# ScalarE takes the last low words and all high-part casts, early softmax sums go two units at a time, and one FFN stage changes its rank

## The chip, the core and the metric

The kernel runs on one core of a Trainium2 chip. Its time is the device time of one execution, in microseconds; a kernel is told by the median of several. Engines: PE (TensorE) multiplies, DVE (VectorE), ACT (ScalarE) and POOL (GpSimd) work on elements, SP (SyncE) issues nearly all DMAs. Each engine takes its instructions strictly in the order of its own queue, so an instruction that waits holds up everything behind it.

## The reference

Windowed attention, then a feed-forward net (FFN) with a rational activation:

```
scores = q @ k.T / 8 + bias        # batch 4, heads 8, 768 positions, head_dim 64; bias falls with distance
keep   = first 8 keys, or the 96 last positions before the query
a      = softmax(where(keep, scores, -1e9))
x      = (a @ v) as (3072 tokens, 512)
h      = x @ w_in                  # 512 x 2048
g      = (a0 + a1 h + a2 h^2 + a3 h^3) / (1 + |b0||h| + |b1|h^2 + 1e-6)
out    = g @ w_out                 # 2048 x 512
```

The weights lie in memory as 64-bit numbers.

## The kernel before

**Tiling.** The 3072 tokens are 12 chunks of 256. A chunk has 8 attention units (two heads of 128 tokens; u = 0 to 95) and 8 FFN steps (256 of the 2048 hidden columns; f = 0 to 95). Attention runs ahead of the FFN: step f of the FFN stands some 10 to 13 units behind.

**An attention unit.** Transposes of q and k (L385), copies out of PSUM (L396), scores (L428), mask and row maximum on DVE (L461), the exponential with its row sums on ACT (L471), then `st_sums`: two tiny DVE instructions, a sum of the two partial sums of each head (L476) and a reciprocal (L478). POOL divides the row by it (`st_norm`, L487; units 0 to 7 don't, their factor is multiplied in at L551). PE transposes the result (`tp`, L503), ACT copies it out (L506), PE multiplies with v (L529), and ACT and DVE make x (L550 and L551 for chunk 0, L558 and L559 after). Units 0 to 23 (`PLAIN = 24`) go in pairs and in plain fp32; the units behind them go one by one. The sums of four units lie side by side in the tile `stats`.

**An FFN step.** PE makes `h` (L263 in fp32 for chunk 0, L271 with high and low parts for the others) in one of two PSUM banks. ACT reads `h` three times (`ew1`, L295 to L297: tiles fu, fa, fs), DVE twice (`ew2`, L302 and L303, into fu), and POOL adds fa and fs (L304). ACT makes a reciprocal q by logarithm and exponential (`ew3`, L311, L312), DVE finishes fu (`ew4`, L316 to L318), and PE multiplies it with w_out (`ffn2`, L342 for chunk 0, L347 after). The two PSUM banks tie the steps: `h` of step f+2 can only start when L297 and L303 of step f have read theirs.

**Weights.** They come in 32 pieces of 128x512 numbers, 16 of w_in (w1_...) and 16 of w_out (w0_...). A DMA (L183) brings a piece's two 32-bit words into a raw buffer `r...`; there are six such buffers, so the piece six later is fetched when the last reader, L209, is done. `decode` makes fp32 of it: ACT takes the magnitude of the top word (L202), POOL the bits that the low word adds (L206; on ACT, L204, where the piece's number is in `LOW_A`, which is piece 0 alone), and DVE puts them together (L207) and sets the sign (L209). The first 20 pieces keep the magnitude in a PSUM bank (`m0` to `m19`), the last 12 in SBUF. Chunk 0 uses the fp32 pieces. For the other chunks `split_w` makes a rounded high part (L222: on DVE for the 16 even numbers in `HI_V`, on ACT for the 16 odd ones) and a low part by subtraction (L223, on POOL or DVE).

**What sets the order.** A scheduler places the instructions when the program is built: `on` and `ffn` give every stage a place 1000 t + PRI_A[stage] (PRI from chunk 1 of the FFN on), smaller first, and a model of the engines' times decides among what is ready. Within a turn t, decoding has 1850 and `ew2` has 2400.

Of the kernel before, what the change touches and what calls it, by code (L numbers as in the profile page):

```python
# [15 lines left out]
ALU = mybir.AluOpType  # L16
# [18 lines left out]
PLAIN = 24  # L35
# [4 lines left out]

SPLITS = {4: 0, 5: 2, 6: 4, 7: 8, 8: 12, 9: 16, 10: 19, 11: 22, 12: 25, 13: 28, 14: 32}

LOW_A = (0,)
BANKS = "hrhaa" * 2 + "raa" * 3 + "r" + " " * 12
HI_V = (0, 2, 4, 6, 8, 10, 12, 14, 16, 18, 20, 22, 24, 26, 28, 30)
LO_V = (13, 15, 17, 19, 21, 23, 25, 27, 29, 31)


PRI = dict(load=0, score=50, soft=100, sums=120, ffn1a=150, qkT=200, pv=250, qkE=300, x=350, split=400, ew3=450, norm=500,
           ffn1b=550, ew1=600, ew4=650, ew2=700, ffn2a=750, pT=800, ffn2b=850, dec=900, wsplit=990)  # L50
PRI_A = dict(PRI, ffn1a=800, pv=1250, qkT=-150, qkE=-100, sums=950, x=1300, split=-700, ew3=2400, norm=1800, ffn1b=900, ew1=1050,
             ew4=850, ew2=2400, ffn2a=-400, pT=850, ffn2b=2050, dec=1850, wsplit=1090)


def positions(nc, rel, key, q0, k0):
# [51 lines left out]
def tile_kernel(ctx: ExitStack, tc: tile.TileContext, q, k, v, n_global, n_local,  # L107
                w_in, w_out, ca, cb, out):
    nc = tc.nc
# [49 lines left out]
    full = {}  # L159
    hi = {}  # L160

    def piece(dt, key):
        return wide.tile([P, 2 * TOK], dt, tag="w", name=f"w{'_'.join(map(str, key))}{'f' if dt is F32 else 'h'}",
                         bufs=NCT * DF // (2 * TOK) + NFT + 1)

    def w_lo(key):
        if key[0]:
            return win_l[:, key[1], key[2] * 2 * TOK:(key[2] + 1) * 2 * TOK]
        return wout_l[:, key[1], :]
# [15 lines left out]
    def decode(key):  # L185
# [16 lines left out]
        nc.scalar.activation(out=mag, in_=raw[:, :, 1], func=AF.Abs, scale=2.0 ** -112)  # L202
        if n in LOW_A:
            nc.scalar.activation(out=low, in_=half, func=AF.Copy, scale=2.0 ** -13, bias=FLOOR)  # L204
# [14 lines left out]

    def split_w(key):  # L220
        hi[key] = piece(FR, key)
        (nc.vector.tensor_copy if len(hi) - 1 in HI_V else nc.scalar.copy)(out=hi[key], in_=full[key])  # L222
        (nc.vector if len(hi) - 1 in LO_V else nc.gpsimd).tensor_tensor(  # L223
            out=w_lo(key), in0=full[key], in1=hi[key], op=ALU.subtract)

# [10 lines left out]
    stats = const.tile([P, 4, 8], F32, name="stats")  # L236
# [135 lines left out]
    prob = {}  # L372
# [99 lines left out]
                                 accum_out=st[:, 2 + 2 * x:3 + 2 * x])  # L472

    def st_sums(u):
        st = prob[u][1]
        nc.vector.tensor_reduce(out=st[:, 6:8], in_=st[:, 2:6].rearrange("p (x w) -> p x w", w=2), op=ALU.add,  # L476
                                axis=mybir.AxisListType.X)
        nc.vector.reciprocal(out=st[:, 6:8], in_=st[:, 6:8])  # L478

    def st_norm(u):  # L480
        if u < DIVIDED:
# [83 lines left out]
    def windowed(lates):  # L565
# [37 lines left out]
        for t in range(NU + LAG + F2 + 1):  # L603
# [5 lines left out]
            def on(name, fn, u, *args, ffn=False, more=0):  # L609
                if 0 <= u < NU:  # L610
                    tc.cur_priority = int(base + when[ffn] + pri[ffn][name] + more)
                    fn(u, *args)
# [9 lines left out]
            def behind(n):  # L622
                past = t - n - 1
                return [past] if past >= PLAIN else [t - 1, t] if t % 2 and t < PLAIN else []
# [9 lines left out]
            for u in behind(1):  # L634
                on("score", st_score, u)
                on("soft", st_soft, u)
                on("sums", st_sums, u)
            if t == PLAIN:
                scope.close()
                pl.late = lates.enter_context(tc.tile_pool(name="late", bufs=1))  # L640
# [41 lines left out]
            if step:  # L682
                for n, key in enumerate(list(full)[SPLITS.get(f - 1, 0):SPLITS.get(f, 0)]):
                    tc.cur_priority = int(base + when[True] + pri[True]["wsplit"] + 4 * n)
                    split_w(key)
# [95 lines left out]
    with ExitStack() as es:  # L781
        pl.ldp = es.enter_context(tc.tile_pool(name="ldp", bufs=2))
        pl.att = es.enter_context(tc.tile_pool(name="att", bufs=2))
        pl.ffn = es.enter_context(tc.tile_pool(name="ffn", bufs=2))
        pl.ps_h = es.enter_context(tc.tile_pool(name="ps_h", bufs=2, space=PSUM))
        pl.ps_o = es.enter_context(tc.tile_pool(name="ps_o", bufs=2, space=PSUM))
        pl.ps_r = es.enter_context(tc.tile_pool(name="ps_r", bufs=1, space=PSUM))
        pl.ps_t = es.enter_context(tc.tile_pool(name="ps_t", bufs=3, space=PSUM))
        with ExitStack() as lates:
            windowed(lates)  # L790
# [53 lines left out]
```

## Time and profile before

| | |
|---|---|
| median of 3 runs | 755.57 us (755.1 to 756.39) |
| the profiled execution | 755.76 us, its span 754.0 us (1.76 us lie around it) |
| busy: PE, DVE, ACT, POOL | 723.2, 600.8, 570.2, 452.6 us |
| granted TensorE clock, mean | 0.986 |

The profiled execution lies 0.19 us above the median. A busy PE is not PE at its peak, and idle time of an engine that is not the bottleneck costs nothing. In the trace the numbers of tiles are left out: `w_2f` of an L263 is w1_0_2f to w1_3_2f, `fu` any of fu0 to fu95.

### The profile page before, as it was taken

What the parts mean: (1) busy time and instruction counts of PE and PEld (TensorE: products, weight loads), DVE (VectorE), ACT (ScalarE), POOL (GpSimd) and SP (SyncE); (2) the same over time, 40 slices, a digit from 0 to 9 for tenths busy, and PEclk for the clock granted to TensorE, in tenths of its full rate; (3) what the DMA queues carried; (4) which work ended last, traced back from release to release, by engine and by line L of the source; (5) the groups of instructions that cost most, each with busy time, mean ns of one, the idle gap of its engine ahead of it and who ended that gap; (6) DMA issues with size and microseconds to landing.
All of it is one profiled execution on the core that took longest, in us unless ns stands there. A gap on an engine that the chain in (4) does not pass through costs nothing.

```text
span 754.0 us, 15278 instructions
## 1 busy us (share of the span) xinstructions
PE 723.2 (96%) x5026; PEld 626.1 (83%) x5026; DVE 600.8 (80%) x1435; ACT 570.2 (76%) x1253; POOL 452.6 (60%) x498
## 2 busy tenths in 40 slices
PE   5898799999999999999999999999999999999996
PEld 3574466888888988998998998998988989998995
DVE  6889955779788798878788888888888888876665
ACT  5888466787887878878877878877878877875764
POOL 3377676776577566656557666665666575664441
PEclk9998899999999999999999999999999999999998
DMA  9986100114433534434434333433434433210000
GB/s 266 341 266 196 35 23 21 50 44 111 135 99 103 144 101 119 124 102 103 120 98 129 101 100 113 121 106 91 127 92 122 117 99 98 81 50 1 29 2 33
DMA packets 123581, 79.49 MB, mean 105 GB/s; under 512 B 82532, under 2 KB 104036, under 8 KB 123492
## 3 DMA queue, kind: packets, MB, share of 16 engines
q1 hardware_dynamic: 122288, 77.89, 36.1%
q8 instruction: 42, 0.69, 0.4%
q10 hardware_dynamic: 1204, 0.52, 0.3%
q14 instruction: 47, 0.39, 0.2%
HBM read 35.92 MB, written 6.29 MB: 56 GB/s over the span
## 4 chain that ended last, share of the span: by engine, by line
PE 85%; DVE 6%; ACT 3%; DMA 2%; issue 2%; POOL 1%; SPq 1%; POOLq 0%; ACTq 0%; DVEq 0%
PE h L271 32%; PE acc L347 31%; PE o L529 5%; PE s L448 4%; PE h L263 3%; PE tp L503 3%; PE acc L342 3%; PE tk L385 2%; PE s L428 2%; DMA r<-in_moe_w_in_dram 1%; ACT pr L471 1%; DVE pr L461 1%; ACT m L202 1%; DVE m L207 1%; DVE fu L316 0%
## 5 line engine op out<-in xcount | busy, mean ns | idle before, releaser
L487 POOL TENSOR_SCALAR pr<-pr,stats 128x256 f32<-128x256 f32 (+1 forms) x176 | 155.3, 895 | 93.1 <-DVE stats L478 47.8
L271 PE MATMUL h<-xh,win_l 128*128 128x256 f32 x704 | 198.2, 281 | 0.0
L304 POOL TENSOR_TENSOR fa<-fa,fs 128x512 f32<-128x512 f32 x95 | 123.8, 1303 | 82.1 <-ACT fs L297 75.0
L347 PE MATMUL acc<-wout_l,g 128*128 128x512 f32 x352 | 139.5, 396 | 0.0
L327 POOL TENSOR_TENSOR g<-fu,g 128x512 fp32r<-128x512 f32 x87 | 112.8, 1297 | 43.8 <-ACT g L326 29.1
L271 PEld LDWEIGHTS h<-xh,win_l 128*128 128x128 f32 x704 | 133.1, 189 | 2.0 <-issue 1.0
L295 ACT ACTIVATE fu<-h,coef 128x512 f32<-128x512 f32 (+1 forms) x97 | 75.1, 774 | 46.5 <-PE h L271 37.4
L471 ACT ACTIVATE pr<-pr,stats 128x256 f32<-128x256 f32 (+1 forms) x192 | 92.7, 485 | 22.6 <-DVE stats L461 21.8
L302 DVE TENSOR_TENSOR fu<-fu,h 128x512 f32<-128x512 f32 (+1 forms) x97 | 65.7, 677 | 40.5 <-ACT fs L297 40.2
L316 DVE SCALAR_TENSOR_TENSOR fu<-fu,coef,q 128x512 f32<-128x512 f32 (+1 forms) x97 | 71.6, 738 | 32.6 <-ACT q L312 30.9
L311 ACT ACTIVATE fs<-fa,coef 128x512 f32<-128x512 f32 (+1 forms) x97 | 69.6, 717 | 26.8 <-POOL fa L304 25.2
L347 PEld LDWEIGHTS acc<-wout_l,g 128*128 128x128 f32 x352 | 66.2, 188 | 12.0 <-issue 0.2
L303 DVE SCALAR_TENSOR_TENSOR fu<-fu,coef,h 128x512 f32<-128x512 f32 (+1 forms) x97 | 71.7, 739 | 2.0
L405 ACT ACTIVATE kq<-tk 64x256 fp32r<-64x256 f32 x144 | 54.3, 377 | 24.6 <-DVE kq L406 12.1
L317 DVE SCALAR_TENSOR_TENSOR q<-fa,coef,q 128x512 f32<-128x512 f32 (+1 forms) x97 | 72.2, 744 | 0.0
L406 DVE SCALAR_TENSOR_TENSOR kq<-tk,kq 64x256 fp32r<-64x256 f32 x144 | 60.7, 422 | 9.2 <-ACT kq L405 5.1
L318 DVE SCALAR_TENSOR_TENSOR fu<-q,fu 128x512 f32<-128x512 f32 (+1 forms) x97 | 66.2, 682 | 1.7
L296 ACT ACTIVATE fa<-h,coef 128x512 f32<-128x512 f32 (+1 forms) x97 | 65.5, 676 | 1.1 <-PE acc L342 0.8
L297 ACT ACTIVATE fs<-h,coef 128x512 f32<-128x512 f32 (+1 forms) x97 | 66.2, 682 | 0.1
L326 ACT CAST g<-fu 128x512 fp32r<-128x512 f32 (+1 forms) x89 | 54.9, 616 | 14.0 <-DVE fu L318 13.3
L506 DVE COPY pT<-tp 128x512 f32<-128x512 f32 (+1 forms) x75 | 48.4, 645 | 19.4 <-PE tp L503 18.3
L312 ACT ACTIVATE q<-fs 128x512 f32<-128x512 f32 (+1 forms) x97 | 57.1, 589 | 4.4 <-DVE stats L478 3.6
(255 smaller groups left out, 1978.4 us busy)
## 6 DMA issues: line engine op xcount, KB each, us to landing
pm<-pr SPq DMA_DIRECT2D x60, 256.0 KB
mv<-nat SPq DMA_DIRECT2D x36, 256.0 KB
qT<-kq SPq DMA_DIRECT2D x144, 64.0 KB
r<-in_moe_w_in_dram SPq DMA_DIRECT2D x16, 512.0 KB
r<-in_moe_w_out_dram SPq DMA_DIRECT2D x16, 512.0 KB
nat<-in_q_dram SPq DMA_DIRECT2D x48, 128.0 KB
vt<-in_v_dram SPq DMA_DIRECT2D x48, 128.0 KB
nat<-in_k_dram SPq DMA_DIRECT2D x46, 128.0 KB
```

The costliest lines, as they stand in the source:

```text
L271: nc.tensor.matmul(out=hps[f][:, y, :], lhsT=w[:, fs], rhs=x[:, ct, :], start=(n == 0), stop=(n == 3 * NCT - 1))
L295: nc.scalar.activation(out=u, in_=h, func=AF.Identity, scale=a3, bias=a2)
L297: nc.scalar.activation(out=s, in_=h, func=AF.Square, scale=b1)
L303: nc.vector.scalar_tensor_tensor(out=u, in0=u, scalar=a1, in1=h, op0=ALU.add, op1=ALU.mult)
L304: side(f).tensor_tensor(out=a, in0=a, in1=s, op=ALU.add)
L311: nc.scalar.activation(out=s, in_=a, func=AF.Ln, bias=q1)
L316: nc.vector.scalar_tensor_tensor(out=u, in0=u, scalar=a0, in1=r, op0=ALU.add, op1=ALU.mult)
L317: nc.vector.scalar_tensor_tensor(out=r, in0=a, scalar=q1, in1=r, op0=ALU.add, op1=ALU.mult)
L327: side(f).tensor_tensor(out=g[:, 1, ys], in0=u, in1=g[:, 0, ys], op=ALU.subtract)
L347: nc.tensor.matmul(out=acc, lhsT=gs[f][:, z, y, ts], rhs=w, start=(ft == 0 and n == 0), stop=(ft == NFT - 1 and n == 2))
L471: nc.scalar.activation(out=d, in_=d, func=AF.Exp, scale=-1.0, bias=st[:, x:x + 1], accum_out=st[:, 2 + 2 * x:3 + 2 * x])
L487: nc.gpsimd.tensor_scalar(out=d, in0=d, scalar1=st[:, 6 + x:7 + x], scalar2=None, op0=ALU.mult)
```

## The change

Five edits:

- `LOW_A` has pieces 20 to 31 too: their low words are made on ACT (L204) instead of POOL (L206).
- `HI_V` is gone: all 32 high parts are cast on ACT.
- `st_sums` for units 0 to 23 is called once for a pair and handles both in one sum and one reciprocal.
- `ew2` has 1700 instead of 2400 in `PRI_A`, ahead of decoding's 1850.
- The call of `st_sums` moves to the odd unit of the pair.

```diff
-LOW_A = (0,)
+LOW_A = (0, *range(20, 32))
-HI_V = (0, 2, 4, 6, 8, 10, 12, 14, 16, 18, 20, 22, 24, 26, 28, 30)
 PRI_A = dict(PRI, ffn1a=800, pv=1250, qkT=-150, qkE=-100, sums=950, x=1300, split=-700, ew3=2400, norm=1800, ffn1b=900, ew1=1050,
-             ew4=850, ew2=2400, ffn2a=-400, pT=850, ffn2b=2050, dec=1850, wsplit=1090)
+             ew4=850, ew2=1700, ffn2a=-400, pT=850, ffn2b=2050, dec=1850, wsplit=1090)
@@ split_w
-        (nc.vector.tensor_copy if len(hi) - 1 in HI_V else nc.scalar.copy)(out=hi[key], in_=full[key])
+        nc.scalar.copy(out=hi[key], in_=full[key])
@@ st_sums
-        st = prob[u][1]
-        nc.vector.tensor_reduce(out=st[:, 6:8], in_=st[:, 2:6].rearrange("p (x w) -> p x w", w=2), op=ALU.add,
+        n = 2 if u < PLAIN else 1
+        st = stats[:, u % 4:u % 4 + n]
+        nc.vector.tensor_reduce(out=st[:, :, 6:8], in_=st[:, :, 2:6].rearrange("p u (x w) -> p u x w", w=2), op=ALU.add,
                                 axis=mybir.AxisListType.X)
-        nc.vector.reciprocal(out=st[:, 6:8], in_=st[:, 6:8])
+        nc.vector.reciprocal(out=st[:, :, 6:8], in_=st[:, :, 6:8])
@@ windowed
-                on("sums", st_sums, u)
+                if u >= PLAIN or u % 2:
+                    on("sums", st_sums, u - (u < PLAIN))
```

In the changed kernel the lines from 46 to 473 have a number smaller by one (L263 is L262 there). The text goes on with the numbers of before.

The scheduler makes new queues of it. PE, in the FFN of chunk 0: `h4` and `h5` are the hidden columns of steps 4 and 5, `acc0_0` and `acc0_1` the output rows, to which step 2 adds fu2. Before, right behind the eight rows of h4:

```order
L263 MATMUL h5_952<-x0_282,w1_0_2f_545 128x256
L263 MATMUL h5_952<-x0_282,w1_1_2f_553 128x256
L263 MATMUL h5_952<-x0_282,w1_2_2f_488 128x256
L263 MATMUL h5_952<-x0_282,w1_3_2f_496 128x256
L342 MATMUL acc0_0_736<-w0_4f_605,fu2_724 128x512
L342 MATMUL acc0_0_736<-w0_5f_613,fu2_724 128x512
L342 MATMUL acc0_1_753<-w0_4f_605,fu2_724 128x512
L342 MATMUL acc0_1_753<-w0_5f_613,fu2_724 128x512
```

PE in the changed kernel, from the last row of h4:

```order
L262 MATMUL h4_854<-x0_278,w1_3_2f_488 128x256
L341 MATMUL acc0_0_724<-w0_4f_595,fu2_712 128x512
L341 MATMUL acc0_0_724<-w0_5f_603,fu2_712 128x512
L341 MATMUL acc0_1_741<-w0_4f_595,fu2_712 128x512
L341 MATMUL acc0_1_741<-w0_5f_603,fu2_712 128x512
L262 MATMUL h5_936<-x0_278,w1_0_2f_535 128x256
L262 MATMUL h5_936<-x0_278,w1_1_2f_543 128x256
```

The four rows with fu2 have moved ahead of h5.

DVE at the same place. L303 with fu3 is the last reader of h3, whose bank h5 needs; L318 with fu2 makes what the four rows of PE need. Before:

```order
L302 TENSOR_TENSOR fu3_821<-fu3_821,h3_805 128x512
L207 SCALAR_TENSOR_TENSOR w0_13f_1003<-w0_13f_1003,r0_13_1004 128x512
L316 SCALAR_TENSOR_TENSOR fu2_724<-fu2_724,coef_63,q2_810 128x512
L317 SCALAR_TENSOR_TENSOR q2_810<-fa2_725,coef_63,q2_810 128x512
L476 TENSOR_REDUCE stats_64<-stats_64 128x2
L209 SCALAR_TENSOR_TENSOR w0_11f_924<-r0_11_925,w0_11f_924 128x512
L476 TENSOR_REDUCE stats_64<-stats_64 128x2
L209 SCALAR_TENSOR_TENSOR w0_12f_996<-r0_12_997,w0_12f_996 128x512
L207 SCALAR_TENSOR_TENSOR w0_14f_1070<-w0_14f_1070,r0_14_1071 128x512
L303 SCALAR_TENSOR_TENSOR fu3_821<-fu3_821,coef_63,h3_805 128x512
L209 SCALAR_TENSOR_TENSOR w0_13f_1003<-r0_13_1004,w0_13f_1003 128x512
```

DVE in the changed kernel:

```order
L206 SCALAR_TENSOR_TENSOR w0_13f_987<-w0_13f_987,r0_13_988 128x512
L301 TENSOR_TENSOR fu3_807<-fu3_807,h3_791 128x512
L317 SCALAR_TENSOR_TENSOR fu2_712<-q2_796,fu2_712 128x512
L476 TENSOR_REDUCE stats_64<-stats_64 128x2x2
L206 SCALAR_TENSOR_TENSOR w0_14f_1054<-w0_14f_1054,r0_14_1055 128x512
L208 SCALAR_TENSOR_TENSOR w0_13f_987<-r0_13_988,w0_13f_987 128x512
L206 SCALAR_TENSOR_TENSOR w0_15f_1061<-w0_15f_1061,r0_15_1062 128x512
L302 SCALAR_TENSOR_TENSOR fu3_807<-fu3_807,coef_63,h3_791 128x512
```

L318 with fu2 (here L317) now stands ahead of L303 with fu3 (here L302), and ahead of L303 stand three instructions more: that one, L209 of w0_13 and L207 of w0_15.

ACT some 25 us earlier, where the decoding of pieces 19 to 24 starts (m19 is piece 19). Before:

```order
L558 CAST xh1_680<-o8_670 128x2x128
L471 ACTIVATE pr10_628,stats_64<-pr10_628,stats_64 128x256
L471 ACTIVATE pr11_635,stats_64<-pr11_635,stats_64 128x256
L471 ACTIVATE pr10_628,stats_64<-pr10_628,stats_64 128x256
L471 ACTIVATE pr11_635,stats_64<-pr11_635,stats_64 128x256
L202 ACTIVATE m19_695<-r0_7_693 128x512
L202 ACTIVATE w0_8f_756<-r0_8_757 128x512
```

ACT in the changed kernel:

```order
L203 ACTIVATE r0_8_745<-r0_8_745 128x512
L558 CAST xh1_668<-o8_658 128x2x128
L470 ACTIVATE pr10_618,stats_64<-pr10_618,stats_64 128x256
L203 ACTIVATE r0_9_752<-r0_9_752 128x512
L470 ACTIVATE pr11_623,stats_64<-pr11_623,stats_64 128x256
L470 ACTIVATE pr10_618,stats_64<-pr10_618,stats_64 128x256
L470 ACTIVATE pr11_623,stats_64<-pr11_623,stats_64 128x256
L310 ACTIVATE fs1_648<-fa1_647,coef_63 128x512
L203 ACTIVATE r1_0_3_759<-r1_0_3_759 128x512
L203 ACTIVATE r1_1_3_766<-r1_1_3_766 128x512
L294 ACTIVATE fu2_712<-h2_693,coef_63 128x512
L295 ACTIVATE fa2_713<-h2_693,coef_63 128x512
```

Behind these come L396 for unit 12 and then L202 of m19: four of the new L204 (here L203) and the pair of L396 now stand ahead of it.

## Rows read from the trace of the kernel before

**Rows 1.** Stages: us, busy us of each engine (instructions), granted clock, DMA share, GB/s

```profile
60.00:80.00 20.00, 13.62 (x59) 8.46 (x57) 20.00 (x33) 13.92 (x30) 13.22 (x13) 0.83 0.58 190
...
100.00:300.00 200.00, 197.79 (x1369) 166.62 (x1369) 158.72 (x395) 157.08 (x353) 133.32 (x143) 1.00 0.33 89
300.00:700.00 400.00, 400.00 (x2980) 363.83 (x2979) 325.68 (x773) 312.38 (x680) 243.15 (x261) 1.00 0.35 99
```

**Rows 2.** Waits of PE, first 100 us: who for whom, us, times, longest

```profile
PE h L263 <- DVE fu L303: 5.6, 1, 5.6
PE acc L342 <- DVE fu L318: 1.7, 1, 1.7
```

**Rows 3.** Waits of PE from 100 us to the end, the longest

```profile
PE acc L347 <- POOL g L327: 1.5, 2, 1.2
```

**Rows 4.** Timeline of PE: start, us, line, op, tiles, count, idle before

```profile
73.13 3.62 PE L263 MATMUL h<-x,w_2f 128*128 128x256 f32 x16
82.37 6.35 PE L263 MATMUL h<-x,w_2f 128*128 128x256 f32 x16 [5.62 <-DVE fu L303]
88.56 1.02 PE L342 MATMUL acc<-w_4f,fu 128*128 128x512 f32 x2
...
92.00 0.82 PE L503 MATMUL tp<-ident,pr 128*128 128x128 f32 x6
```

**Rows 5.** Short stages, columns as in rows 1

```profile
80.00:82.00 2.00, 0.00 (x0) 0.00 (x0) 2.00 (x5) 0.38 (x1) 0.00 (x0) 0.73 0.00 0
...
84.00:86.00 2.00, 2.00 (x7) 1.55 (x6) 2.00 (x4) 1.75 (x3) 2.00 (x3) 0.50 0.00 0
```

**Rows 6.** Timeline of DVE

```profile
39.51 0.68 DVE L209 SCALAR_TENSOR_TENSOR w_2f<-r,m 128x512 int32<-128x512 int32 x1
...
55.29 0.70 DVE L207 SCALAR_TENSOR_TENSOR m<-m,r 128x512 int32<-128x512 int32 x1 [0.22 <-ACT m L202]
...
60.13 1.13 DVE L209 SCALAR_TENSOR_TENSOR w_9f<-r,w_9f 128x512 int32<-128x512 int32 x1
...
64.09 1.76 DVE L209 SCALAR_TENSOR_TENSOR w_3f<-r,w_3f 128x512 int32<-128x512 int32 x1
...
75.08 0.87 DVE L222 CAST w_0h<-w_0f 128x512 fp32r<-128x512 f32 x1
...
81.58 0.74 DVE L303 SCALAR_TENSOR_TENSOR fu<-fu,coef,h 128x512 f32<-128x512 f32 x1
```

**Rows 7.** Line L478: engine, op, count, shortest, median, longest in ns

```profile
L478 DVE RECIPROCAL stats<-stats x96: 144/158/169, 12.4 to 672.9; 128x2 f32<-128x2 f32 x96
```

**Rows 8.** Timeline of ACT

```profile
9.42 0.64 ACT L204 ACTIVATE r<-r 128x512 int32<-128x512 uint16 x1
9.96 0.39 ACT L471 ACTIVATE pr<-pr,stats 128x128 f32<-128x128 f32 x1
...
54.58 0.62 ACT L202 ACTIVATE m<-r 128x512 f32<-128x512 f32 x1
...
56.41 0.66 ACT L396 ACTIVATE kF<-tk 128x256 f32<-128x256 f32 x2 [0.61 <-PE tk L385]
```

**Rows 9.** Timeline of POOL

```profile
59.59 1.12 POOL L206 TENSOR_SCALAR r<-r 128x512 int32<-128x512 uint16 x1
...
63.70 1.59 POOL L304 TENSOR_TENSOR fa<-fa,fs 128x512 f32<-128x512 f32 x1
```

**Rows 10.** Groups from 54 to 90 us: busy us, mean ns, idle before

```profile
L206 POOL TENSOR_SCALAR r<-r 128x512 int32<-128x512 uint16 x9 | 7.1, 787 | 7.2 <-DMA r<-in_moe_w_out_dram 2.6 <-DMA r<-in_moe_w_in_dram 2.3 <-DVE fu L318 1.1
```

**Rows 11.** L207, then L209, of DVE in one stage: us, busy us (instructions)

```profile
55.20:82.40 27.20, 9.67 (x12) 0.85 0.54 171
55.20:82.40 27.20, 10.28 (x11) 0.85 0.54 171
```

**Rows 12.** L222 in one stage: busy us of DVE, then of ACT

```profile
90.00:250.00 160.00, 7.69 (x14) 8.71 (x14) 1.00 0.28 73
```

**Rows 13.** All engines in the stage of decoding, columns as in rows 1

```profile
57.00:85.00 28.00, 19.24 (x73) 12.09 (x72) 27.96 (x46) 18.31 (x38) 17.79 (x17) 0.81 0.50 156
```

## The prediction

> **What bounds the kernel now.** I read the stages first [rows 1]. From 300 to 700 us PE is busy all the time; from 100 to 300 us it lacks 2.2 us of 200. DVE, ACT and POOL have room in both (DVE 81%, ACT 78% in the later one). So work taken from DVE or POOL there buys nothing, and work given to ACT costs nothing as long as it isn't late. Only one stage is different: from 60 to 80 us PE is busy for 13.6 of 20 us, DVE for all 20, and the clock is 0.83. The waits of PE name the place [rows 2]: 5.6 us for L303, once, and 1.7 us for L318. Behind 100 us its longest wait is 1.2 us, for POOL's L327 [rows 3]. The timeline of PE shows what the long wait costs [rows 4, 5]: the 16 matmuls of h5 start at 82.37 and take 6.35 us, those of h4 took 3.62. In between PE did nothing, and the granted clock fell from 2.4 to 1.2 GHz (0.73 from 80 to 82 us, 0.50 from 84 to 86). Wait and slow clock together are 5.6 + 2.7 = 8.3 us, the most that can be won here.
>
> Why L303 is late: DVE works without a pause from 55.29 us, where the decoding of the last 13 pieces starts (L207 of m19, behind L202 of m19 on ACT, 54.58), to the end of L303 at 82.32 [rows 6, 8]. These 27.0 us hold 12 L207 and 11 L209 with 9.7 + 10.3 us [rows 11], most of the stage.
>
> **The change part by part.** My marker is the moment when PE has h5 and the four rows with fu2 behind it and turns to `tp`: 92.00 us before [rows 4]. From there on PE is nearly full, so what is won at the marker is won at the end, unless something new is late.
>
> *Start of DVE's stretch.* It moves back. L551 of the last x of chunk 0 now stands behind L209 (0.68) and the reciprocal (0.16) which it led before [rows 6, 7]: PE starts h0 some 0.8 us later. On ACT, four new L204 stand ahead of L202 of m19. The one L204 in the trace took 0.64 us, and the next instruction started 0.54 us behind its start [rows 8]; I take 0.55, so 2.2 us. The pair of L396 (0.66, 0.55 net) stands ahead of it too. Sum 0.8 + 2.2 + 0.5 = 3.5 us; I see nothing that hides it, because DVE has nothing else in its queue there. Bounds: 2.2 (the L204 alone) and 5 (if one of them waits for its DMA).
>
> *DVE from there to the end of L303 with fu3.* Three more instructions stand ahead of it, L318, L209 and L207, each 0.68 to 0.70 long with 0.6 from start to start: + 1.8. The cast of w1_2_0 goes (0.87, 0.8 net) and one of the tiny sums (0.1): - 0.9. Then the stretching: a quiet L207 or L209 takes 0.68, so 23 of them make 15.6 us; the rows have 19.95 [rows 11], so 4.3 us are added by other work; the long rows are of pieces from 20 on, whose operands all lie in SBUF. Beside a POOL L206 the excess is small (60.13: 1.13, + 0.45, beside 59.59) and beside a POOL L304 large (64.09: 1.76, + 1.08, beside 63.70) [rows 6, 9]. Of the nine L206 from 54 to 90 us [rows 10] I take three or four to meet such an instruction, for some 1.5 us; they go to ACT, away from DVE. The L304 and L223 stay, as many as before, and with them the other 2.8. Sum: 27.0 + 1.8 - 0.9 - 1.5 = 26.4. So L303 ends at 55.3 + 3.5 + 26.4 = 85.2 instead of 82.3. With no stretching at all it would be 82.2.
>
> The Trainium skill has a rule on this (SBUF — State Buffer, section SBUF: two separate sides): a GpSimd instruction and a VectorE instruction with two SBUF inputs lock a port pair against each other for a whole instruction. The excess beside L304 looks like it, that beside L206 is less than a whole instruction. By the rule alone the L206 could give back up to their whole length, 7.1 us; this is the first rival below.
>
> *PE.* The four rows with fu2 now stand ahead of h5, and they need L318 with fu2, which now ends ahead of L303 by L303, two L207, one L209 and a tiny sum, 2.6 us: at 82.6. They take 3.4 us (88.56 to 92.00): 86.0. The bank of h3 is free since 85.2, so h5 starts without a wait and ends at 89.5 at the full clock. The marker comes 2.5 us earlier than at 92.00. What was a wait of 5.6 us becomes one of 3 to 4 us ahead of the rows with fu2, and the clock, which before fell some 4 us into the idle time (from 76.75; the mean of 0.73 puts the step near 80.9), mostly stays up. If it falls again, the 2.7 us are lost again and the gain is nothing. If DVE is not stretched, the marker comes 3 us earlier still: 5.5.
>
> *The other edits.* The sums save 12 times two tiny instructions, 0.3 us a pair, on DVE ahead of 240 us. In the first 55 us DVE waits for DMA and ACT anyway, and later PE is full: nothing. Fourteen of the casts move from DVE to ACT behind 90 us, 7.7 us less on one and about 8.7 more on the other [rows 12]. ACT is busy 157 of 200 us from 100 to 300 [rows 1], so it goes to 83%: hidden behind PE, with the 1.2 us wait for L327 as the nearest row of what lateness costs there, in either direction. POOL and DVE get lighter where PE still lacks 2.2 us; I take half a microsecond of gain.
>
> *Sum.* 755.76 - 2.5 - 0.5 = 752.8 for the profiled execution; it lay 0.2 above its median, so **752.6 us**.
>
> **Rivals.**
>
> *A. DVE gets free of POOL.* If most of the stretching goes with the L206, and the clock stays up, L318 ends some 3 us earlier and the marker comes 5.5 us earlier, more if ACT's L204 cost less than I take: 755.6 - 6.5 = 749. For it: DVE is the engine that is full there. Against it: the long rows stand beside L304 and L223, which stay.
>
> By the Trainium skill's rule of the lock, up to 7.1 us would leave DVE instead of 1.5, and the time would be about this.
>
> *B. The wait has only moved.* L318 is later than I think by 1 to 2 us (each microsecond costs one), or the clock falls in the new wait: the gain is 0 to 1 us, the time 755. For it: DVE starts 3.5 us late, and PE still runs dry once.
>
> *C. ACT becomes the one that all wait for, and the time gets longer.* ACT is busy 18.3 of 28 us from 57 to 85 [rows 13]. Eight L204 and two casts more make it 24; and it inherits, in its queue, the waits for the pieces' DMAs (POOL's L206 waited 4.9 us for them [rows 10]), which move back with the L209 that frees a raw buffer. L204 of w0_15 is then ready at about 81 by my count, and DVE wants it at about 83.9: from 2.8 us of extra lateness on, every microsecond is PE's. With all 4.9 us L303 ends 2.1 later and the clock falls in the longer wait (2.7): 752.6 + 4.8 = 757.4, or 758 with some lateness behind 100 us. Against it: those waits have ACT's idle 9.7 us to fall into.
>
> The Trainium skill speaks against this part of the change (ScalarE: Activation LUTs, section Rules for kernel authors: adds and multiplies belong on VectorE). The trace agrees on the direction for casts, 0.62 us on ACT and 0.55 on DVE on the mean [rows 12], but the price matters only where ACT is late.
>
> **How the numbers follow.** The forecast 0.52 (750.5 to 754.5), A 0.18 (747 to 750.5), B 0.18 (754 to 756.5), C 0.12 (757 to 760). What a measurement of this kernel can tell from no change is about 0.2%, 1.5 us. Faster than 754.1: A and nine tenths of the forecast, 0.18 + 0.47 = 0.65. Within: the rest of the forecast and B, 0.23. Slower than 757.1: C, 0.12. The range leaves out the lower half of A and C: 748.5 to 756.8.
>
> **What would show it.** In the profile after: L207 of m19 on DVE at 58 to 59 us (not 55.3), L303 with fu3 ending at 84 to 86, L342 with fu2 ahead of h5 with a wait of 3 to 4 us in front, h5 with no wait and 3.6 us long, `tp` behind them at 89 to 90. L207 and L209 beside L304 still at 1.7 us. Then PE full from 100 us on, with waits of no more than 2 us in sum. It is wrong if h5 still waits for L303, if the clock is at half under the rows with fu2, or if ACT's L204 show waits for DMA ahead of L303.

## The result: 0.6% slower, and the profile after

| | before | after |
|---|---|---|
| median of 20 runs each | 755.49 us | 760.03 us |
| lowest to highest | 754.37 to 756.83 | 754.77 to 764.66 |
| ratio, 95% interval | | 1.0058 (1.0043 to 1.0073) |
| profiled execution, its span | 755.76, 754.0 | 761.17, 759.3 |

The change makes the kernel 4.5 us slower, where 752.6 was forecast. It also spreads the runs over 10 us instead of 2.5. Lines 46 to 473 of the kernel before have a number one lower in the changed kernel (L303 is L302, L318 is L317, L263 is L262, L342 is L341, L204 is L203, L206 on POOL is L205).

The stages of the changed kernel, columns as in [rows 1]:

```profile
40.00:60.00 20.00, 17.05 (x95) 13.63 (x94) 13.18 (x32) 16.51 (x39) 12.00 (x15) 1.00 0.76 241
60.00:80.00 20.00, 16.15 (x65) 9.59 (x64) 19.20 (x35) 19.22 (x40) 6.61 (x7) 0.83 0.62 195
80.00:100.00 20.00, 16.52 (x55) 9.90 (x55) 15.18 (x23) 11.88 (x23) 13.44 (x12) 0.91 0.04 10
100.00:300.00 200.00, 195.57 (x1338) 163.95 (x1338) 151.90 (x373) 161.23 (x363) 134.89 (x143) 1.00 0.32 87
300.00:700.00 400.00, 400.00 (x2992) 363.77 (x2988) 325.56 (x773) 312.13 (x681) 243.10 (x261) 1.00 0.36 100
```

From 60 to 80 us PE is busy 2.5 us longer than before, as intended. But from 40 to 60 us, where before it was busy all the time, it now lacks 3 us, and from 100 to 300 us it lacks 4.4 of 200 (2.2 in [rows 1]). From 300 to 700 us it is full in both. Before:

```profile
40.00:60.00 20.00, 20.00 (x104) 15.19 (x103) 16.97 (x39) 17.39 (x37) 16.83 (x20) 1.00 0.76 231
```

The place of the forecast, on PE (columns as in [rows 4]):

```profile
77.89 3.62 PE L262 MATMUL h<-x,w_2f 128*128 128x256 f32 x16
84.99 1.45 PE L341 MATMUL acc<-w_4f,fu 128*128 128x512 f32 x2 [3.48 <-DVE fu L317]
86.24 1.91 PE L341 MATMUL acc<-w_5f,fu 128*128 128x512 f32 x2
87.95 1.58 PE L341 MATMUL acc<-w_4f,fu 128*128 128x512 f32 x2
89.37 1.02 PE L341 MATMUL acc<-w_5f,fu 128*128 128x512 f32 x2
90.23 3.62 PE L262 MATMUL h<-x,w_2f 128*128 128x256 f32 x16
93.68 0.60 PE L503 MATMUL tp<-ident,pr 128*128 128x128 f32 x4
```

The order is the forecast one: the rows with fu2 stand ahead of h5 with a wait of 3.5 us in front, and h5 runs in 3.62 us without a wait. But three of the four pairs with fu2 ran partly at 1.2 GHz (1.45, 1.91 and 1.58 for 1.02), and all of it is late: the marker is at 93.68, not at 89.5 (before: 92.00).

Why it is late, on DVE, then on POOL and ACT:

```profile
41.43 0.39 DVE L551 TENSOR_TENSOR x<-x,o 128x256 f32<-128x256 f32 x1
46.10 1.45 DVE L206 SCALAR_TENSOR_TENSOR m<-m,r 128x512 int32<-128x512 int32 x2 [4.28 <-POOL r L205]
```

```profile
41.68 3.64 POOL L487 TENSOR_SCALAR pr<-pr,stats 128x256 f32<-128x256 f32 x4 [2.93 <-DVE stats L478]
45.41 2.93 POOL L205 TENSOR_SCALAR r<-r 128x512 int32<-128x512 uint16 x4
```

```profile
9.91 0.62 ACT L201 ACTIVATE m<-r 128x512 f32<-128x512 f32 x1 [2.29 <-DMA r<-in_moe_w_in_dram]
56.52 0.72 ACT L310 ACTIVATE fs<-fa,coef 128x512 f32<-128x512 f32 x1
57.14 1.26 ACT L203 ACTIVATE r<-r 128x512 int32<-128x512 uint16 x2
58.27 0.78 ACT L294 ACTIVATE fu<-h,coef 128x512 f32<-128x512 f32 x1
58.94 0.69 ACT L295 ACTIVATE fa<-h,coef 128x512 f32<-128x512 f32 x1
60.04 0.65 ACT L201 ACTIVATE m<-r 128x512 f32<-128x512 f32 x1
```

The same places before, on ACT, POOL and DVE:

```profile
8.85 0.64 ACT L202 ACTIVATE m<-r 128x512 f32<-128x512 f32 x1 [1.29 <-DMA r<-in_moe_w_in_dram]
39.05 0.65 POOL L206 TENSOR_SCALAR r<-r 128x512 int32<-128x512 uint16 x1 [1.81 <-DMA r<-in_moe_w_in_dram]
40.44 3.63 POOL L487 TENSOR_SCALAR pr<-pr,stats 128x256 f32<-128x256 f32 x4 [0.75 <-DVE stats L476]
40.81 0.70 DVE L207 SCALAR_TENSOR_TENSOR m<-m,r 128x512 int32<-128x512 int32 x1 [0.28 <-ACT m L202]
```

With one sum for two units, all four L487 of the pair become ready at once. They stand at the head of POOL's queue, wait there 2.93 us for the reciprocal (L478), work for 3.64, and the low word of r1_1_2, which before stood ahead of them (39.05), starts at 45.41. DVE idles 4.28 us for it; before, the same L207 started at 40.81, with 0.28 us of idle time. Behind it in DVE's queue stand L301 and L302 of the FFN, which come at 49.25 and 51.05 (44.52 and 45.24 before).

ACT then comes to the L201 of m19 at 60.04 (54.58 before), so DVE's stretch starts at 60.77 instead of 55.29. Of these 5.5 us ACT's four low words take 2.3 (from start to start, as all that follow) and L395 takes 0.5. Another 1.9 us are L310, L294 and L295 of the FFN: before, they ran ahead of the exponentials (50.98, 50.30 and 51.59), now they stand behind them and ahead of m19, as the printed order of ACT shows. The last 0.8 us is what ACT was late at the cast L558 (53.73; 52.33 before), less the first low word, which stands ahead of it. The first weight piece landed 1.06 us later, too (9.91; 8.85 before).

PE's idle rows from 100 to 300 us that are longer than 0.2 us, all of them:

```profile
212.34 0.54 PE L384 MATMUL tk<-ident_r,mv 128*128 128x128 f32 x4 [0.78 <-DVE pT L506]
216.22 0.50 PE L346 MATMUL acc<-w_4h,g 128*128 128x512 f32 x1 [0.78 <-ACT g L325]
245.06 1.97 PE L529 MATMUL o<-pT,vt 128*64 128x128 f32 x32 [0.98 <-DVE stats L460]
265.21 0.35 PE L447 MATMUL s<-kq,qT 128*128 128x256 f32 x1 [1.57 <-DMA qT<-kq]
```

Four waits of 0.8 to 1.6 us, two for DVE, one for ACT and one for a DMA: no one engine is the bound, and none of them stands in [rows 3].

**An account of PE's time.** For the experiments I split each profiled span into five parts. *Idle* is the length of a stage less PE's busy time. *Half clock* is half of PE's busy time at 1.2 GHz, the time ahead of the first granted clock in the trace counted with it, since its rows are as long (before, four L385 take 1.11 us at 8.49, ahead of the first record, and 0.66 at 23.58; a pair of L341 takes 1.02 at 2.4 GHz and 1.91 at 1.2). *Long rows* is how much PE's rows from 100 to 300 us add to the busy time above the median of their line (118 ns for an L271, 234 for an L347). What is left should be the same for every kernel if the three explain the time:

| profile | idle to 100 us | half clock to 100 us | idle 100 to 300 | long rows 100 to 300 | left |
|---|---|---|---|---|---|
| before | 21.9 | 11.3 | 2.2 | -0.1 | 718.6 |
| after | 23.0 | 11.8 | 4.4 | 1.5 | 718.5 |
| u_ew2 (after once more) | 21.6 | 10.3 | 4.2 | 1.3 | 718.7 |
| d_low | 19.8 | 11.3 | 4.4 | 1.6 | 719.8 |
| n_half | 19.2 | 10.9 | 0.6 | -1.1 | 718.3 |
| s_half | 19.2 | 11.0 | 4.8 | 0.9 | 718.7 |
| s_late | 22.2 | 11.8 | 4.6 | -1.5 | 718.7 |
| c_half | 18.7 | 11.9 | 0.8 | -1.9 | 718.1 |

In 19 of the 20 profiles of this study what is left is 718.1 to 720.4 us (u_cast, with half clock behind 100 us too, has 716.6). So the whole effect lies in two numbers: what PE loses up to 100 us (before 33.2, after 34.8) and from 100 to 300 us (before 2.1, after 5.9). This is bookkeeping: PE has the same 5026 rows in every kernel, so the table tells where the time went and not why. "Long rows" is the roughest column, since it also moves by some tenths with the number of short L529 that fall into the window (208 before, 188 after).

### The profile page after: what moved, and what is told of

It is laid out like the page before. It is cut to its first block, busy times and chain, and to the rows that moved or that the text cites. A ratio compares the mean times of both kernels' runs of the same rounds, so it can differ in the third digit from the quotient of the medians.

```text
span 759.3 us, 15246 instructions
## 1 busy us (share of the span) xinstructions
PE 724.8 (95%) x5026; PEld 626.5 (83%) x5026; DVE 589.0 (78%) x1396; ACT 582.6 (77%) x1280; POOL 443.0 (58%) x486
## 4 chain that ended last, share of the span: by engine, by line
PE 82%; ACT 6%; DVE 4%; issue 2%; DMA 1%; POOL 1%; SPq 0%; DVEq 0%; POOLq 0%; ACTq 0%
PE h L270 31%; PE acc L346 31%; PE o L529 5%; PE s L447 4%; PE tp L503 3%; PE acc L341 3%; PE h L262 2%; PE tk L384 1%; ACT pr L470 1%; PE s L427 1%; DVE q L316 1%; ACT fu L294 1%; DVE fu L317 1%; ACT r L203 0%; DVE fu L315 0%
## 5 line engine op out<-in xcount | busy, mean ns | idle before, releaser
L487 POOL TENSOR_SCALAR pr<-pr,stats 128x256 f32<-128x256 f32 (+1 forms) x176 | 155.4, 895 | 82.0 <-DVE stats L478 43.9
L303 POOL TENSOR_TENSOR fa<-fa,fs 128x512 f32<-128x512 f32 x95 | 123.8, 1304 | 109.8 <-ACT fs L296 99.8
L294 ACT ACTIVATE fu<-h,coef 128x512 f32<-128x512 f32 (+1 forms) x97 | 75.2, 775 | 51.5 <-PE h L270 41.6
L301 DVE TENSOR_TENSOR fu<-fu,h 128x512 f32<-128x512 f32 (+1 forms) x97 | 65.6, 676 | 35.2 <-ACT fs L296 35.0
L310 ACT ACTIVATE fs<-fa,coef 128x512 f32<-128x512 f32 (+1 forms) x97 | 69.7, 719 | 27.8 <-POOL fa L303 26.4
L404 ACT ACTIVATE kq<-tk 64x256 fp32r<-64x256 f32 x144 | 54.4, 378 | 25.2 <-PE tk L384 11.8
L302 DVE SCALAR_TENSOR_TENSOR fu<-fu,coef,h 128x512 f32<-128x512 f32 (+1 forms) x97 | 71.6, 738 | 2.0
L405 DVE SCALAR_TENSOR_TENSOR kq<-tk,kq 64x256 fp32r<-64x256 f32 x144 | 60.6, 422 | 10.4 <-ACT kq L404 6.0
L317 DVE SCALAR_TENSOR_TENSOR fu<-q,fu 128x512 f32<-128x512 f32 (+1 forms) x97 | 66.2, 682 | 1.7
L295 ACT ACTIVATE fa<-h,coef 128x512 f32<-128x512 f32 (+1 forms) x97 | 65.7, 677 | 0.0
```

The costliest lines, as they stand in the source:

```text
L294: nc.scalar.activation(out=u, in_=h, func=AF.Identity, scale=a3, bias=a2)
L302: nc.vector.scalar_tensor_tensor(out=u, in0=u, scalar=a1, in1=h, op0=ALU.add, op1=ALU.mult)
L303: side(f).tensor_tensor(out=a, in0=a, in1=s, op=ALU.add)
L310: nc.scalar.activation(out=s, in_=a, func=AF.Ln, bias=q1)
L317: nc.vector.scalar_tensor_tensor(out=u, in0=r, scalar=2.0, in1=u, op0=ALU.subtract, op1=ALU.mult, reverse0=True)
L487: nc.gpsimd.tensor_scalar(out=d, in0=d, scalar1=st[:, 6 + x:7 + x], scalar2=None, op0=ALU.mult)
```

## The experiments

Ratios are against the kernel before on the same chip, with their 95% interval. In the names d_ is the kernel before with one part of the change, u_ the changed kernel with one part undone; n_ and c_ start from the kernel before, s_ and f_ from the changed one, with the edits that their diffs show.

**Part by part.** Four theories stood first: S, the paired sums (by POOL's queue); L, the low words on ACT; C, the casts on ACT; D, luck of the one profile.

```diff
 d_sums: st_sums and its call as in the change, nothing else
-LOW_A = (0,)
+LOW_A = (0, *range(20, 32))                            # d_low alone
-        (nc.vector.tensor_copy if len(hi) - 1 in HI_V else nc.scalar.copy)(out=hi[key], in_=full[key])
+        nc.scalar.copy(out=hi[key], in_=full[key])     # d_cast alone
 u_sums: the changed kernel with st_sums and its call of before
```

> The kernel before with one part of the change alone: the early sums and reciprocals for two units at once. Theory S (the sums are the cause): with one sum for two units, POOL's four L487 stand at the head of POOL's queue, ahead of the low word of r1_1_2, and wait there for the pair's reciprocal (in the changed kernel 2.93 us of waiting and 3.64 us of work, 41.68 to 45.41), so DVE's L207 of that piece starts at about 45 us with 3 to 4.5 us of idle time in front (40.81 before, no idle time), and the time is 758 to 760 us. Theory L (the low words on ACT are the cause): 755.5, as before. Theory C (the casts are the cause): 755.5. Theory D (the 1.06 us by which the first weight piece landed later in the changed kernel's profile, 9.91 against 8.85, and the clock behind it): no more than 1 us in either direction, with the wide spread of the changed kernel.

Measured 756.93, 1.0014 (1.0002 to 1.0027). The wait of S is there to the hundredth:

```profile
44.77 1.45 DVE L207 SCALAR_TENSOR_TENSOR m<-m,r 128x512 int32<-128x512 int32 x2 [4.28 <-POOL r L206]
57.14 0.70 DVE L207 SCALAR_TENSOR_TENSOR m<-m,r 128x512 int32<-128x512 int32 x1 [1.05 <-POOL r L206]
```

But it costs 1.1 us, not 2.5 to 4.5: DVE's stretch starts 1.85 us later than before (57.14), no more. On ACT it is the same three FFN instructions that stand behind the exponentials and ahead of m19 (54.02 to 55.87, 1.85 us). S names a real wait and overprices it.

> The kernel before with one part alone: ScalarE makes the low words of pieces 20 to 31. Theory S: the start of DVE's stretch (L207 of m19) moves from 55.3 to about 57.5 us only (four L204 at 0.55), POOL gives way, the time is 753 to 756. Theory L: the four L204 and those behind them hold up ACT's other work, L207 of m19 comes at 59 to 61 us, PE waits and falls to the half clock under the rows with fu2, 758 to 760. Theories C and D: 755.5 within 1.

Measured 761.63, 1.0076 (1.0060 to 1.0092): above even L's 758 to 760. Yet L207 of m19 came at 56.71, only 1.4 us later (L: 59 to 61), and PE lost 2.1 us less up to 100 us than before. The loss is behind 100 us, where L didn't look (6.0 against 2.1). The profiled execution was the fastest of the six, 758.75, so half of the 5.8 us is in no profile.

> The kernel before with one part alone: all casts to high parts on ScalarE. Theory C: PE's waits from 100 to 300 us grow from 1.9 to 4 us and more, the time is 757.5 to 759. Theories S, L and D: nothing ahead of 85 us changes, the time is 755.5 within 1.

Measured 754.00, 0.9974 (0.9961 to 0.9987): faster. PE lacks 0.45 us from 100 to 300 us instead of 2.2. C has fallen.

> The changed kernel with the sums and reciprocals taken unit by unit as before, all else changed. Theory S: POOL's low word of r1_1_2 is ahead of its L487 again, DVE has no idle time of 4 us at 42 us, the marker comes at 89 to 91 us and the time is 752.5 to 755.5. Theory L: 758 to 760, as the changed kernel. Theory C: 757 to 760, with PE's waits of 4 us behind 100 us. Theory D: 759 to 761.

Measured 756.34, 1.0006 (0.9992 to 1.0020): 3.7 us below the changed kernel (2.0 below its second measurement, u_ew2), and in the range of none of the four theories. DVE's wait of 4.28 us is gone, as S has it; but the L206 of r1_1_2 came at 44.12 all the same, with 0.28 us of idle time, and the stretch started at 60.13. So the paired sums are one way to a late start and not the only one. And low words and casts together cost 0.5, alone +5.8 and -1.9: the parts don't add.

**The other half of the table.**

```diff
 u_low: the changed kernel with LOW_A = (0,)
 u_cast: the changed kernel with HI_V and the cast of before
 u_ew2: the changed kernel with ew2=2400
 f_l15: the changed kernel with LOW_A = (0, 15, *range(20, 32))
```

> The changed kernel with the low words of pieces 20 to 31 back on POOL (paired sums and casts stay). The first four runs gave, against the kernel before, +1.1 us for the sums alone, -1.9 for the casts alone, +5.8 for the low words alone. Theory A (each part has a price of its own, the low words on ACT cost most): -0.8, so about 755 us, 5 less than the changed kernel. Theory P (the parts only shuffle the order, and what counts is how the queues happen to meet; prices don't add, since low words and casts together were +0.5 and not +3.9): anything from 753 to 761, with no relation to the sum.

Measured 754.75, 0.9988 (0.9976 to 1.0000), as A has it.

> The changed kernel with every second cast back on VectorE (paired sums and low words stay). Theory A: 1.1 + 5.8, so about 762.5 us, with PE idle for more than 4 us behind 100 us. Theory P: anything from 753 to 761.

Measured 764.50, 1.0119 (1.0103 to 1.0134), the slowest of all, above A's 762.5 and P's 761; PE lost 12.4 us from 100 to 300 us.

> The changed kernel with the fourth part undone, ew2 back at 2400. The order of instructions on each engine stays what it is in the changed kernel, so this is that kernel once more: 760 us, and a second profile of it. Theory D (the changed kernel's loss is luck of its one profile: the first piece landing 1 us late, the clock): the first L206 on DVE comes at 10 and not at 11 us, the low words' waits differ, and the idle time of PE behind 100 us is not 4.4 us again. Theories S, L and A: the same waits stand in the same places (DVE idle 4 us ahead of L206 of r1_1_2, PE 4.4 us idle from 100 to 300 us).

Measured 758.32, 1.0041 (1.0026 to 1.0056). The fourth part of the change moves no instruction: PE, DVE, ACT and POOL run the order of the changed kernel from the first row to the last, so this is that kernel again. The same four waits stand in the same places:

```profile
209.51 0.54 PE L384 MATMUL tk<-ident_r,mv 128*128 128x128 f32 x4 [0.88 <-DVE pT L506]
213.39 0.50 PE L346 MATMUL acc<-w_4h,g 128*128 128x512 f32 x1 [0.76 <-ACT g L325]
242.25 1.97 PE L529 MATMUL o<-pT,vt 128*64 128x128 f32 x32 [0.98 <-DVE stats L460]
262.39 0.35 PE L447 MATMUL s<-kq,qT 128*128 128x256 f32 x1 [1.20 <-DMA qT<-kq]
```

So they are not luck, and D has fallen for this half. In the other half it has something: here the rows with fu2 ran at 2.4 GHz and the marker came at 90.73, with the first piece landing as late (9.80):

```profile
83.74 1.12 PE L341 MATMUL acc<-w_4f,fu 128*128 128x512 f32 x2 [2.85 <-DVE fu L317]
84.70 1.02 PE L341 MATMUL acc<-w_5f,fu 128*128 128x512 f32 x2
87.28 3.62 PE L262 MATMUL h<-x,w_2f 128*128 128x256 f32 x16
90.73 0.60 PE L503 MATMUL tp<-ident,pr 128*128 128x128 f32 x4
```

One order of rows, two executions, 2.95 us between the markers and 3.2 us between the spans; by the table, half of that is clock (11.8 and 10.3) and half is idle time (23.0 and 21.6). Each run's mean granted clock is on record, too: of the 20 runs of the changed kernel the fastest, 754.77, had 0.999 and the slowest, 764.66, had 0.982, and over all 20 time and clock are correlated by -0.68. So the clock goes with about half of the wide spread; where the rest comes from is not shown.

> The changed kernel with one more low word on ScalarE, that of piece 15 (r1_1_2), which in the changed kernel stands behind the four L487 on POOL. Theory S (this wait starts the lateness): DVE's idle time of 4.3 us at 42 us goes, L207 of m19 comes 2 to 3 us earlier, at 58 us, the marker at 91 to 92, and the time is 757 to 758.5. Theory A, in which the low words on ACT are the price and the sums only 1.1: 759 to 760. Theory P: it is another shuffle, anything from 754 to 762.

Measured 756.60, 1.0020 (1.0006 to 1.0035): 1.7 to 3.4 us better than the changed kernel, a little more than S gave; the stretch started at 57.80. The loss up to 100 us falls to 29.0, that behind stays at 5.9.

All eight combinations of the three parts, in us against before (the changed kernel by its two runs): sums +1.1, casts -1.9, low +5.8, sums and casts -0.9, low and casts +0.5, sums and low +8.9, all three +2.7 and +4.5. Low words cost in each of the four pairs, so theory A (a price for each part) looked good.

**Is it ACT's work, POOL's relief, or the order?**

```diff
 n_odd: HI_V = (1, 3, ..., 31)                          # before: (0, 2, ..., 30)
+        if n >= 20:                                    # n_abs2: the Abs once more
+            nc.scalar.activation(out=mag, in_=raw[:, :, 1], func=AF.Abs, scale=2.0 ** -112)
-        else:                                          # n_skip: no low word from 20 on,
+        elif n < 20:                                   # and in1=bits there
             nc.gpsimd.tensor_scalar(out=low, in0=half, ...
 n_half: LOW_A = (0, *range(26, 32))
```

> The kernel before with the odd pieces' casts on VectorE and the even ones' on ScalarE, instead of the other way round: as many instructions on each engine, in another order from about 85 us on. Theory A (the low words on ACT have a price): 755.5 within 1, with PE 2 us idle from 100 to 300 us. Theory P (any shuffle of the order costs or gains some us): 1.5 us or more away from 755.5, in either direction.

Measured 757.75, 1.0025 (1.0016 to 1.0034): as many casts on each engine (the scheduler also put one copy of an output on DVE instead of ACT), and 2.0 us more. Theory P is right that the order alone moves the time.

> The kernel before with the Abs of pieces 20 to 31 done twice on ScalarE: 12 instructions of 0.55 more on ACT, where the low words would stand; POOL keeps the low words. Theory A1 (the price is ACT's work, 6.6 us between 53 and 85 us): 759 to 762, as with the low words on ACT (761.6). Theory A2 (the price comes with what is taken from POOL): 755.5 within 1. Theory P: no relation.

Measured 754.17, 0.9984 (0.9974 to 0.9993): A1 has fallen. Twelve more instructions on ACT at the disputed place cost nothing.

> The kernel before without the low words of pieces 20 to 31: POOL loses these 12 instructions, ACT gets none; VectorE ORs the shifted word with itself, so these 12 weight pieces are not the reference's. Theory A1: 753 to 755.5, since POOL and DVE only get freer. Theory A2: 759 to 762. Theory P: no relation.

Measured 756.53, 1.0007 (0.9993 to 1.0022): between the two, nearer to A1's end, so A2 has fallen too. Neither ACT's work nor POOL's relief shows as the price. But each of the two kernels also has an order of its own (on PE from 64 and 68 us on), and the order alone moved n_odd by 2 us, so a price of that size could hide in either.

> The kernel before with the low words of the last 6 pieces (26 to 31) on ScalarE. Theory A1 or A2 (a price for each): half of 5.8, so 757.5 to 759.5. Theory P: anything from 753 to 762.

Measured 750.43, 0.9937 (0.9920 to 0.9954): 5.3 us faster, where half of the price was expected. Theory A has fallen.

**Which pieces?** Theory E: the first of the twelve are dear.

```diff
 n_half1: LOW_A = (0, *range(20, 26))
 n_nine:  LOW_A = (0, *range(23, 32))
 s_half:  the changed kernel with LOW_A = (0, *range(26, 32))
 c_half:  d_cast with LOW_A = (0, *range(26, 32))
```

> The kernel before with the low words of pieces 20 to 25 alone on ScalarE (the first six of the twelve). The last six alone gave 750.4, all twelve 761.6. Theory E (the first six are the dear ones: they stand in ACT's queue ahead of the L202 of m19 and among the exponentials and copies of attention, 53 to 60 us, and what they hold up is missing later): 759 to 764, with PE 5 us or more short from 100 to 300 us. Theory P (no piece has a price of its own; each edit deals the order behind 100 us anew): anything from 750 to 762, the loss from 100 to 300 us with no relation to the number of low words on ACT.

Measured 758.02, 1.0027 (1.0017 to 1.0036): dear, but by 2.2 us and up to 100 us (36.5), with nothing lost behind (-0.1). E had it the other way round.

> The kernel before with the low words of pieces 23 to 31 on ScalarE (nine of the twelve). Theory E: between the two, 754 to 758. Theory P: anything from 750 to 762.

Measured 749.94, 0.9919 (0.9903 to 0.9935): 11.7 us below all twelve. In this company pieces 20, 21 and 22 decide, and not by a price for each.

> The changed kernel with the low words of pieces 20 to 25 back on POOL: only 26 to 31 on ScalarE, paired sums and all casts on ScalarE as in the change. Theory E: the dear part of the change is gone, 750 to 754. Theory P: anything from 750 to 762. In both the time follows what PE lacks ahead of 100 us and from 100 to 300 us: about 719 us and those two.

Measured 755.40, 0.9995 (0.9983 to 1.0006): E has missed. Up to 100 us PE lost 30.2 us instead of 31.9 and 34.8. Behind it lost 5.7, and the four waits came back:

```profile
208.31 0.54 PE L384 MATMUL tk<-ident_r,mv 128*128 128x128 f32 x4 [1.30 <-DVE pT L506]
212.20 0.50 PE L346 MATMUL acc<-w_4h,g 128*128 128x512 f32 x1 [0.78 <-ACT g L325]
241.04 1.97 PE L529 MATMUL o<-pT,vt 128*64 128x128 f32 x32 [0.98 <-DVE stats L460]
260.82 0.35 PE L447 MATMUL s<-kq,qT 128*128 128x256 f32 x1 [1.20 <-DMA qT<-kq]
```

The reason is in the instruction streams: from 134 us of the changed kernel's trace on, PE, DVE, ACT and POOL run the very order of the changed kernel.

> The kernel before with all casts on ScalarE and the low words of pieces 26 to 31 there too, sums unit by unit: the two parts that were faster alone (754.0 and 750.4). If gains add: 748 to 749.5. Theory E: 748 to 752. Theory P: anything from 750 to 760.

Measured 749.40, 0.9908 (0.9890 to 0.9925): the lowest median, though not to be told from n_nine's. Here the two gains nearly add (-1.9 and -5.3 alone, -6.4 together). It shows the forecast order as it was meant, with the wait ahead of fu2 and none ahead of h5:

```profile
80.37 1.12 PE L341 MATMUL acc<-w_4f,fu 128*128 128x512 f32 x2 [3.16 <-DVE fu L317]
81.33 1.82 PE L341 MATMUL acc<-w_5f,fu 128*128 128x512 f32 x2
82.95 1.91 PE L341 MATMUL acc<-w_4f,fu 128*128 128x512 f32 x2
85.83 3.62 PE L262 MATMUL h<-x,w_2f 128*128 128x256 f32 x16
89.28 0.60 PE L502 MATMUL tp<-ident,pr 128*128 128x128 f32 x4
```

But the clock fell here, too (the four pairs took 5.24 us). The marker comes at 89.28 because DVE's stretch started at 56.05. Behind 100 us PE is nearly full:

```profile
100.00:300.00 200.00, 199.21 (x1394) 170.59 (x1393) 156.22 (x388) 163.82 (x371) 133.79 (x144) 1.00 0.34 92
```

**The last question: low words, or the order behind 100 us?**

```diff
-LO_V = (13, 15, 17, 19, 21, 23, 25, 27, 29, 31)
+LO_V = (13, 15, 17, 20, 22, 24, 26, 28, 30, 31)        # s_late, in the changed kernel
 c_nine: d_cast with LOW_A = (0, *range(23, 32))
```

> The changed kernel with another choice of the pieces whose low parts VectorE makes: 13, 15, 17, 20, 22, 24, 26, 28, 30, 31 in place of 13, 15, ..., 31; as many on each engine. All rows that the changed kernel runs ahead of about 110 us stand where they stood; behind that, up to about 300 us, the order is dealt anew. Theory O (the late loss belongs to the order of the rows behind 110 us and to no part of the change as such): PE's four waits of the changed kernel (for pT, g, stats and qT, 209 to 262 us) are gone or others, the loss from 100 to 300 us is no longer 5.4 to 5.9 us but anything from -1 to 6, most likely less, and the time 753 to 759. Theory L (ScalarE's low words bring the late loss through the state in which they leave the engines at 100 us): loss and time as in the changed kernel, 758 to 760.

Measured 757.08, 1.0022 (1.0009 to 1.0035), 2.1 us below the mean of the changed kernel's two medians. Up to 100 us it lost 34.0, as that kernel. PE's order differs only from 145 to 342 us (the first difference on any engine is at 142), and there all four waits are gone, with others in their place:

```profile
166.25 0.39 PE L270 MATMUL h<-xh,w_3h 128*128 128x256 f32 x1 [0.98 <-DVE fu L302]
182.90 0.38 PE L270 MATMUL h<-xh,w_0h 128*128 128x256 f32 x1 [1.17 <-DVE fu L302]
197.22 0.39 PE L447 MATMUL s<-kq,qT 128*128 128x256 f32 x1 [1.54 <-DMA qT<-kq]
```

Theory L would have kept the waits, so as it was put it has fallen: which rows wait goes with the order, and a tuple of piece numbers changes it. But the idle time there is as much as ever (4.6); the loss is 3.1 and not 5.5 to 5.9 because the rows are 3 us shorter. And all seven profiles with all twelve low words on ACT have 3.6 to 5.7 us of idle time from 100 to 300 us, whatever else was changed; of the other 13 only d_sums (3.4), c_nine (3.9) and s_half (4.8) have more than 2.2. So Theory O is shown for the waits; that the low words have no part in the late loss is not shown.

The first 142 us are a third execution of the changed kernel's order, with the first weight piece at 9.07. DVE's stretch started there later still:

```profile
61.60 0.70 DVE L206 SCALAR_TENSOR_TENSOR m<-m,r 128x512 int32<-128x512 int32 x1 [3.17 <-ACT m L201]
```

> The kernel before with all casts and the low words of pieces 23 to 31 on ScalarE, the candidate that the runs so far point to (749.9 with these nine alone, 749.4 with the casts and the last six). Theory E (pieces 20 to 22 are the dear ones, the rest pay): 748.5 to 750. Theory O: the order behind 100 us is dealt anew, 748 to 756.

Measured 752.85, 0.9964 (0.9951 to 0.9977): E's 748.5 to 750 is missed: nine low words with the casts are 3.5 us slower than six with them (c_half). Up to 100 us PE lost 30.2, behind it 3.0: its order there is another one.

## Why the prediction was wrong, point by point

The profiled execution was forecast at 752.8 and took 761.17, so 8.4 us are missing: 4.1 up to 100 us and 4.3 behind. The marker's 93.68 against 89.5 makes as much: 2.0 us by the start of DVE's stretch, 0.4 by its length, 1.8 by the clock.

*The step that failed: "from there on PE is nearly full, so what is won at the marker is won at the end, unless something new is late", with half a microsecond of gain for the later stages.* PE's loss from 100 to 300 us grew by 3.8 us in the profiled execution and by 3.4 in the second one. I had counted busy shares there (ACT 83%) and called it hidden. But every edit ahead of 100 us changes the list from which the order behind 100 us is made, and in 20 profiles that stage lost between -1.1 and 12.4 us. s_half and s_late show that the waits go with the order: the same order with the same waits under another start, and other waits in another order under the same start. Why one order is good and another bad I can't say; whether all twelve low words on ACT lead to bad ones stays open, too.

*Start of DVE's stretch: 58 to 59 forecast, 60.77 measured.* The three terms of the sum, 3.5 us, were right in size: low words 2.3 for 2.2, L395 0.5, lateness 0.8. What the sum left out are the 1.9 us of L310, L294 and L295, which the order printed under the change shows between the exponentials and m19. d_sums has these three at the same place and starts 1.85 us late by them. I priced the paired sums at nothing, as DVE work of a tenth of a microsecond; their price is a wait, since POOL's L487 of both units stand ahead of a low word and wait for the pair's reciprocal, and the FFN, which on DVE stands behind the L206 of that low word, comes late (1.1 us of time in d_sums). The late landing of the first piece (8.4 to 9.9 us in the 20 profiles, 9.1 to 9.9 in the three executions of one order) does not explain the start: s_late, with the earliest landing of the three, starts the stretch last, at 61.60. The Trainium skill (TensorE: Matmul & The Clock Gate, section Architectural detail: the array is 16× 32×32, not 1× 128×128) states that GpSimd's queue is strictly first in, first out; the trace agrees: the low word at 45.41 stood behind the L487 that had waited for 2.93 us.

*Length of the stretch: 26.4 forecast, 26.8 measured.* Taken row by row from the timelines, the 22 whole L207 and L209 of before were together 5.1 us longer than 0.68 each, and the 24 L206 and L208 here are 4.1 longer. (My 4.3 from [rows 11] is too small: the last of its 23 rows, at 82.24, lies in that window with 0.16 us only.) So some 1.0 us has gone with POOL's low words, where I took 1.5. Rival A, by which most of the stretching goes, has fallen: some rows, beside POOL's L303 and L222, are as long as ever (groups of DVE from 60.6 to 87.7 us: busy us, mean ns, idle before):

```profile
L208 DVE SCALAR_TENSOR_TENSOR w_11f<-r,w_11f 128x512 int32<-128x512 int32 x1 | 1.8, 1767 | 0.0
L206 DVE SCALAR_TENSOR_TENSOR w_13f<-w_13f,r 128x512 int32<-128x512 int32 x1 | 1.7, 1745 | 0.0
```

The Trainium skill's rule of the port pair (SBUF — State Buffer, section SBUF: two separate sides) would have given back up to 7.1 us by my estimate; the rows here show 1.0.

*The wait on PE: 3 to 4 us ahead of fu2, h5 without one.* Right (3.48). *The clock "mostly stays up": it fell in the profiled execution (1.8 us) and stayed up in the second.* I had named this as what would cost the gain.

*The casts: nothing.* Alone they are a gain of 1.9 us, with the two waits for POOL's g gone ([rows 3]); the order behind them is another one, too.

*Rival C had the sign and nearly the time (757.4 to 758), by the wrong mechanism:* DVE waiting for ACT's last low words. DVE has no idle time from 60.77 to the end of L302 at 87.59, so it never waited for one there, and n_abs2, with as much more work on ACT, is 1.5 us faster than before. *Rival B*, the wait only moved, describes the first 100 us: 34.8 and 31.9 us lost there, 33.2 before.

*The new rank of `ew2`*, one of the five edits, moves nothing (u_ew2): that the rows with fu2 stand ahead of h5 comes from the other parts.

## What to carry to other kernels

Where a scheduler makes the order, the price of an edit is not its instructions: a swap that is neutral for every engine but for one copy cost 0.25% here (n_odd), and three of twelve moved instructions turned a gain of 0.8% into a loss of 0.8%. Forecast such an edit with a range of the size of that lottery, measure several neighbours of it (other pieces, other counts) and keep the best order rather than the best argument; here that is six low words and all casts on ScalarE without the paired sums, 749.40 us or 0.9908 of before (nine low words without the casts, 749.94, are as good within the noise). And if one small result is made for two consumers at once, look at which queue its readers head, and what stands behind them.

## What the hardware showed that I had not expected

One order of rows can meet PE's clock at either level: the same eight rows behind a wait of 3.48 us ran partly at 1.2 GHz (5.24 us for the four pairs), behind one of 2.85 us at 2.4 GHz (3.54). The length of the wait alone doesn't tell which: in c_half the clock fell under them behind 3.16 us (5.24), in s_late, with the changed kernel's order, it stayed up behind 3.24 (85.81 to 89.35, 3.54):

```profile
85.81 1.12 PE L341 MATMUL acc<-w_4f,fu 128*128 128x512 f32 x2 [3.24 <-DVE fu L317]
89.35 3.62 PE L262 MATMUL h<-x,w_2f 128*128 128x256 f32 x16
```

Four waits of PE, two for DVE, one for ACT and one for a DMA, each 0.8 to 1.6 us long, came back in three executions within 0.6 us of their length, in s_half 75 us and more behind the last place where its order differs.
